# Four padding tiles and wider weight rows: every matmul operand 64 bytes past a multiple of 128

## Chip, cores, metric

One core of a Trainium2 chip runs the kernel; the seven others are idle. The metric is the device time of one execution in microseconds, the median of several runs. Beside it stands one profiled execution, from which every view of the trace comes.

## What is computed

Four residual layers in a row on `x` of 2048 positions by 640 features, A, B, A, B, with a layer norm in front of each. A is a sliding dilated attention, B a two-dimensional Fourier mixing done with matmuls. Cut to what matters:

```python
def _A_ref(x, wqkv, wo):                  # H = 32 heads of 20, window W = 8, dilation 2
    q, k, v = split_heads(x @ wqkv)
    kg, vg = k[idx], v[idx]               # 8 positions: pos, pos-2, ..., pos-14
    logits = einsum("bhsd,bhswd->bhsw", q, kg) * scale
    o = einsum("bhsw,bhswd->bhsd", softmax(masked(logits)), vg)
    return merge_heads(o) @ wo

def _B_ref(x, dft_seq_re, dft_seq_im, dft_hid_re, dft_hid_im):
    a = einsum("bsd,ed->bse", x, dft_hid_re)
    b = einsum("bsd,ed->bse", x, dft_hid_im)
    return einsum("ts,bse->bte", dft_seq_re, a) - einsum("ts,bse->bte", dft_seq_im, b)

x = x + _A_ref(_layernorm(x), wqkv, wo)
x = x + _B_ref(_layernorm(x), ...)
x = x + _A_ref(_layernorm(x), wqkv, wo)
x = x + _B_ref(_layernorm(x), ...)
```

## The kernel before

Every float32 operand of a product is kept as two float32r tiles, a high part `hi` and the rest `lo`, and a product runs as three matmuls: hi x hi, hi x lo, lo x hi (`PASSES`, line 213; the second index is that of the moving operand). A matmul has a stationary operand of 128 x 128 and a moving one of 128 x N, and adds into a PSUM bank.

**Layer A** (`layer_a`) goes over four row blocks c of 512 positions (each four tiles j of 128) and four quarters q of the QKV weights. `qkv_mm` (line 347, matmul on 357) makes one tile of 128 positions by 480 columns: 15 matmuls, k = 0 to 4 in each of the three passes, with the stationary tile `s0` to `s3` (the transposed, normalized input of tile j) and the moving tile `r1_q`, the split weights. There are 128 such tiles in the two layers, 1920 matmuls of 480 columns. The attention itself runs on VectorE, GpSimd and ScalarE (lines 422 to 482). `wo_mm` (line 495, matmul on 504) multiplies by `wo` in products of 320 columns. At the end of the layer `z_mm` of `LayerB` (line 903, matmul on 914) already makes the first sequence product of layer B (t = 0), with the moving tile `ct` in `s0` to `s3` and the stationary tile `r1_c`, which now holds the normalized rows of block c. The order in which all engines work in layer A is written out by hand (`PHASES`, `at`).

**Layer B** first runs `zpart` for t = 1 (16 steps s of 15 matmuls of 512 columns, line 914): the moving tile is `s3` for even s and `s0` for odd s, the stationary tile `r1_c` with c = s // 4. Beside it VectorE makes combined inputs (`x_combine`), which are stored to DRAM through two `stg` buffers. Then come three pairs (`pair`), each with three loops of eight iterations of 512-wide products (`product`, matmul on 1081): 18 matmuls an iteration in the first loop, 21 in the second, 15 in the third. Their moving tiles are split DFT rows in `s0`, `s1` or in cells of `r1_2` and `r1_3`, their stationary tiles either a cell of `r1_0` to `r1_3` read where it stands (`x_plain`) or a combined input loaded into a cell of `r1_0` or `r1_1` (`x_slot`; the ring goes over the eight cells of `r1_0` and `r1_1` in loops 1 and 2, two cells an iteration, and over the four of `r1_1` in loop 3). `ymm` (matmul on 992) multiplies by the hidden-dimension matrices in products of 320 columns, with moving tiles in `r2a`, `pr0` to `pr3` and `zo3`. TensorE's order is written by hand; that of the other engines in layer B is left to the tile scheduler.

**Where tiles lie.** A tile is asked for under a tag. All tiles of a tag share one place; the places follow each other in the order in which the tags are first asked for, each rounded up to 32 bytes (per partition), behind an area of 16384 bytes that is reserved for DMA descriptors and 128 bytes of constants. From this follow the addresses before, as remainders:

| tag | holds, as a matmul operand | start | mod 128 |
|---|---|---|---|
| `ident`, `nident` | matrices of transposes and subtractions | 16544, 17056 | 32 |
| `s3` | input tile j = 3, DFT rows | 17568 | 32 |
| `r1_0` | QKV weights q = 0, rows of block 0 in layer B | 22784 | 0 |
| `pr0` | hidden-dimension weights k = 0 | 43264 | 0 |
| `win` (five buffers) | none | 48384 to 62464 | 0 or 64 |
| `pr1` to `pr3` | hidden-dimension weights | 65984 to 76224 | 64 |
| `r1_1`, `r2a`, `r1_2`, `r1_3` | as `r1_0`, and `wo` | 81344 to 147904 | 64 |
| `zo0` to `zo3`, `ot`, `s0`, `s1`, `s2`, `xa` | stationary tiles, DFT rows | behind | 64 |

Inside a tile all matmul operands start at multiples of 128 bytes from the tile's start (a block of 128 float32 is 512 bytes, a weight row of 480 is 1920 = 15 x 128, one of 320 is 1280). Modulo 256 the weight rows of 480 alternate, since 1920 = 7.5 x 256. The places end at 229312 of the 229376 bytes of a partition.

Of the kernel before, what the change touches and what calls it, by code (L numbers as in the profile page):

```python
# [11 lines left out]
F32R = mybir.dt.float32r  # L12
# [14 lines left out]
P = 128  # L27
# [3 lines left out]
KD = D // P  # L31
F = 160
# [42 lines left out]
def tile_layers(ctx: ExitStack, tc: tile.TileContext, x, wqkv, wo, cs, wre, wim, out):  # L75
    nc = tc.nc
# [9 lines left out]
    def nm(base):  # L86
        uid[0] += 1
        return f"{base}_{uid[0]}"

    def T(shape, tag, dt=F32, bufs=1, pool=None):  # L90
        return (pool or sb).tile(shape, dt, tag=tag, name=nm(tag), bufs=bufs)
# [4 lines left out]
    warm = T([P, 1], "warm")  # L96
    nc.vector.memset(warm, 0.0)
    nc.scalar.activation(warm, warm, AF.Exp)
    ident = T([P, P], "ident")
    make_identity(nc, ident)  # L100
    nident = T([P, P], "nident", F32R)
# [6 lines left out]
    mhalf = T([P, 4], "mhalf")  # L108
    nc.gpsimd.memset(mhalf, -0.5)
    mask = T([P, SLOTS], "mask")  # L110
    nc.gpsimd.memset(mask, 0.0)
    nc.gpsimd.memset(mask[0:2, 0:3], NEG)
    nc.gpsimd.memset(mask[0:1, 3:7], NEG)
# [11 lines left out]
    def split(hi, lo, src, neg=False, eng=None):  # L125
        nc.scalar.activation(hi, src, AF.Copy, scale=-1.0 if neg else 1.0)
        if neg:
            nc.vector.scalar_tensor_tensor(lo, src, -1.0, hi.bitcast(F32), op0=ALU.mult, op1=ALU.subtract)
        else:
            (eng or nc.vector).tensor_tensor(lo, src, hi.bitcast(F32), op=ALU.subtract)  # L130
# [57 lines left out]
    def load_x(src, j, tag="xa"):  # L188
        xt = T([P, D], tag, bufs={"xa": 2}.get(tag, 1))
        nc.sync.dma_start(xt, src[:, j, :])  # L190
        return xt
# [10 lines left out]
    def wq_load1(q, k):  # L202
        raw = wtile([P, 3 * F])
        nc.sync.dma_start(raw, wqkv[q][:, k, :])
        return raw

    def a_weights_q(q):
        wt = T([P, 2, KD, 3 * F], f"r1_{q}", F32R)
        for k in range(KD):
            split(wt[:, 0, k], wt[:, 1, k], wq_load1(q, k))  # L210
        return wt
# [25 lines left out]
    def layer_a(li, stats, handoff, prev):  # L237
# [4 lines left out]
        wq = {}  # L242
# [16 lines left out]
        def at(step, phase, fn, *args):  # L259
            plan.setdefault((step, phase), []).append((fn, args))  # L260
# [5 lines left out]
        def x_load(c, j, tag="xa"):  # L266
            xnT[(c, j)] = load_x(xin[c], j, tag)

        def x_stats(c, j, fast=False):
            if j == 0:  # L270
                stats[c] = Stats()
            stats[c].tile(j, xnT[(c, j)], fast)

        def x_fin(c, j):
            stats[c].finish(j, j + 1)

        def x_norm(c, j, fast=False):
            stats[c].apply(j, xnT[(c, j)], fast)

        def xt_pe(c, j, part, bank):  # L280
            if part == 0:
                xnT[(c, j, 1)] = T([P, 2, KD, P], f"s{j}", F32R)
            xnT[(c, j, "p", part)] = t_pe(xnT[(c, j)], part, bank)

        def xt_hi(c, j, part):
            t_hi(xnT[(c, j, 1)], part, xnT[(c, j, "p", part)])

        def xt_lo(c, j, part):
            t_lo(xnT[(c, j, 1)], part, xnT[(c, j, "p", part)])
# [234 lines left out]
            nstats[c].finish(j0, j1)  # L524

        def wq_begin(q):
            wq[q] = T([P, 2, KD, 3 * F], f"r1_{q}", F32R)

        def wq_raw(q):
            if q < 3:  # L530
                if q == 1:
                    wq["raw"] = T([P, 2, KD, 3 * F], "r2a")
                nc.sync.dma_start(wq["raw"][:, q - 1], wqkv[q])
                for k in range(KD):
                    wq[(q, k)] = wq["raw"][:, q - 1, k]
                return
            for i, tag in enumerate(("zo2", "zo3", "ot")):
                k0, k1 = 2 * i, min(2 * i + 2, KD)
                raw = wq_load(q, k0, k1, tag)
                for k in range(k0, k1):  # L540
                    wq[(q, k)] = raw[:, k - k0]
# [26 lines left out]
        def early():  # L568
            def x_get(j):
                x_load(0, j)  # L570
                x_norm(0, j)

            def w0():
                with tc.issue_after(prev.dma.ins):
                    wq[0] = a_weights_q(0)

            def xt(j, part):
                xt_pe(0, j, part, "pq")
                xt_hi(0, j, part)
                xt_lo(0, j, part)  # L580

            prev.pair(
                NPAIR - 1,
                stats,
                {
                    2: lambda: (x_get(0), x_get(1)),
                    4: lambda: xt(0, 0),
                    5: lambda: (xt(0, 1), x_get(2)),
                    6: lambda: xt(1, 0),
                    7: lambda: (w0(), xt(1, 1), x_get(3)),  # L590
                    ("y", 1): lambda: xt(2, 0),
                    ("y", 2): lambda: xt(2, 1),
                    "end": lambda: (xt(3, 0), xt(3, 1)),
                },
            )
            for q in range(1, NQ):
                wq[q] = a_weights_q(q)
# [7 lines left out]

        def prologue_first():
            wq_begin(0)
            for j, (k0, k1) in enumerate(((0, 3), (3, 5))):
                x_load(0, j, f"pr{j}")
                for k in range(k0, k1):  # L610
                    wq[(0, k)] = wq_load1(0, k)
            for j in range(2, NJ):
                x_load(0, j, f"pr{j}")
            for q in (1, 2, 3):
                wq_begin(q)
                wq_raw(q)
            w0 = wq[0]

            def whi(k, eng):
                (eng.tensor_copy if eng is nc.vector else eng.copy)(w0[:, 0, k], wq[(0, k)])  # L620

            def wlo(k, eng):
                eng.tensor_tensor(w0[:, 1, k], wq[(0, k)], w0[:, 0, k].bitcast(F32), op=ALU.subtract)

            def xt_all(j, bank):
                return [(xt_pe, (0, j, i, f"{bank}{i}")) for i in range(2)] + [
                    (f, (0, j, i)) for i in range(2) for f in (xt_hi, xt_lo)
                ]

            x_stats(0, 0, True)  # L630
            x_fin(0, 0)
            for k in range(3):
                whi(k, nc.scalar)
            wlo(0, nc.vector)
            x_norm(0, 0, True)
            wlo(1, nc.gpsimd)
            for i in range(2):
                xt_pe(0, 0, i, f"t{i}")
            for i in range(2):
                xt_hi(0, 0, i)  # L640
            x_stats(0, 1, True)
            wlo(2, nc.gpsimd)
            x_fin(0, 1)
            whi(3, nc.vector)
            whi(4, nc.vector)
            for i in range(2):
                xt_lo(0, 0, i)
            wlo(3, nc.vector)
            wlo(4, nc.vector)
            x_norm(0, 1, True)  # L650
            x_stats(0, 2, True)
            x_fin(0, 2)
            mid[0] = xt_all(1, "aux") + [(x_stats, (0, 3, True)), (x_fin, (0, 3)), (x_norm, (0, 2, True))]
            mid[1] = xt_all(2, "t") + [(x_norm, (0, 3, True)), (zero_rows, ())]
            mid[2] = xt_all(3, "aux")
            for i in range(KD):
                at(LEAD0[0] + 1 + i // 2, "misc", wq_split, 1, i)
                at(LEAD0[0] + 3 + i, "misc", wq_split, 2, i)
                at(LEAD0[0] + 5 + i, "misc", wq_split, 3, i)
# [31 lines left out]
        while len(gs) < NGRP:  # L691
            if st % 2 == 0 and len(tx) < NC * NJ:
                c, j = divmod(len(tx), NJ)
# [114 lines left out]
        with tc.manual_schedule(engines=ENGINES):  # L808
            if first:
                prologue_first()  # L810
            nc.vector.tensor_copy(mk, mask)
            for s in range(LEAD0[0], last + 1):
                for ph in PHASES:
                    for fn, args in plan.pop((s, ph), ()):
                        fn(*args)
            pc_pe(67)
            pc_hi(67)
            pc_lo(67, True)
            wo_mm(c, 2, None, 0, 2, 3)
            wo_mm(c, 3, ("pq", "aux0"))  # L820
            wo_add(c, 2)
            wo_stats(c, 2)
            wo_fin(c, 2, 3)
            if first:
                handoff.c_hl(14)
            handoff.ln_tail(c, 2, xr, nstats)
            wo_add(c, 3)
            handoff.ln_lo(c, 2)
            handoff.z_mm(14, None)
            wo_stats(c, 3)  # L830
            wo_fin(c, 3, 4)
            if first:
                handoff.c_hl(15)
            handoff.ln_tail(c, 3, xr, nstats)
            handoff.ln_lo(c, 3)
            handoff.z_mm(15, None)
# [478 lines left out]
```

## Time and profile before

| | us |
|---|---|
| median of 3 runs | 1810.0 (1809.1 to 1810.69) |
| span of the profiled execution | 1804.2 |
| TensorE matmul busy in it | 1745.8 (97%) |
| VectorE busy | 1392.7 (77%) |
| ScalarE busy | 818.3 (45%) |
| GpSimd busy | 633.5 (35%) |
| DMA moved | 423.59 MB |

The profile is of one execution; its span runs from the first to the last instruction, and the runs' time also holds what lies around it. PE stands for TensorE's matmuls, PEld for its weight loads, DVE for VectorE, ACT for ScalarE, POOL for GpSimd, SP for the engine that issues most DMAs. Matmuls overlap each other in the pipeline, so one record lasts longer than the distance to the next (383 ns on average for a 480-wide one); what counts for the time is the distance from start to start, which a window with a known number of matmuls shows. The chain of waits is followed back from the last instruction: at each step to what released it, or to the instruction before it on the same engine.

### The profile page before, as it was taken

How to read it: one execution, taken by the hardware profiler on the slowest of the kernel's cores; microseconds unless marked ns; L12 is line 12 of the kernel's file. 1: busy time of each engine (PE TensorE's matmuls, PEld its weight loads, DVE VectorE, ACT ScalarE, POOL GpSimd, SP SyncE). 2: the span in 40 equal slices, each digit the busy share in tenths (PEclk: the TensorE clock that was granted, in tenths of full speed). 3: DMA queues.
4: the chain of work that ended last, by engine and by line, in shares of the span. 5: the costliest groups of instructions: out<-in, count | busy, mean ns of one | idle time of the engine just before them, and what ended most of it. 6: DMA issues, size and time to landing. Idle time of an engine off the chain costs nothing.

```text
span 1804.2 us, 26493 instructions
## 1 busy us (share of the span) xinstructions
PE 1745.8 (97%) x8798; PEld 1506.7 (84%) x8798; DVE 1392.7 (77%) x2135; ACT 818.3 (45%) x1708; POOL 633.5 (35%) x591
## 2 busy tenths in 40 slices
PE   9999997988999999999999999999899999999999
PEld 7879886877888888888888888888788888888888
DVE  5899899887767767768739988899777677677673
ACT  5544644544445445445633334444434443443441
POOL 3799898960000000000008987889400000000000
PEclk9999999999999999999999999999999999999999
DMA  6776667648777887888737856687687767776761
GB/s 233 224 264 206 208 206 250 211 150 293 255 261 247 293 267 248 290 269 267 251 124 227 278 184 198 201 299 260 218 295 262 262 223 228 264 232 229 254 209 52
DMA packets 273994, 423.59 MB, mean 235 GB/s; under 512 B 22688, under 2 KB 153248, under 8 KB 273600
## 3 DMA queue, kind: packets, MB, share of 16 engines
q1 hardware_dynamic: 270656, 419.92, 70.1%
q10 hardware_dynamic: 3200, 1.97, 0.4%
q8 instruction: 70, 1.15, 0.3%
q14 instruction: 68, 0.56, 0.1%
HBM read 336.66 MB, written 85.14 MB: 234 GB/s over the span
## 4 chain that ended last, share of the span: by engine, by line
PE 64%; DVE 15%; DMA 9%; POOL 6%; issue 3%; ACT 3%; SPq 0%; DVEq 0%; ACTq 0%; POOLq 0%
PE m L357 15%; PE aux L992 12%; PE t L1081 10%; PE m L1081 10%; PE pq L1081 5%; PE xt L1081 5%; PE aux L504 4%; DMA xc<-stg 4%; DVE pr L426 3%; DVE pr L464 2%; POOL pr L479 2%; DMA win<-cs_in 1%; POOL pr L428 1%; DVE lg L434 1%; POOL r L864 1%
## 5 line engine op out<-in xcount | busy, mean ns | idle before, releaser
L357 PE MATMUL m<-r,s 128*128 128x480 f32 x1920 | 438.8, 383 | 7.4 <-ACT s L227 3.5
L357 PEld LDWEIGHTS m<-r,s 128*128 128x128 f32 x1920 | 356.1, 189 | 63.5 <-ACT s L227 5.1
L1074 ACT CAST r<-win 128x512 fp32r<-128x512 f32 x251 | 153.0, 620 | 171.8 <-DVE win L1110 73.1
L169 POOL TENSOR_TENSOR stats<-stats,mhalf 128x1 f32<-128x1 f32 (+1 forms) x40 | 29.1, 727 | 566.3 <-ACT stats L165 566.2
L992 PE MATMUL aux<-r2a,zo 128*128 128x320 f32 x768 | 226.4, 310 | 0.0
L479 POOL TENSOR_TENSOR pr<-pr 128x640 f32<-128x640 f32 x126 | 203.5, 1615 | 43.1 <-DVE pr L464 42.1
L426 DVE TENSOR_TENSOR pr<-pq,win 128x1280 f32<-128x1280 f32 x128 | 189.8, 1483 | 26.7 <-ACT pq L399 26.5
L992 PE MATMUL aux<-pr,zo 128*128 128x320 f32 x704 | 208.2, 308 | 0.0
L1075 DVE TENSOR_TENSOR r<-win,r 128x512 fp32r<-128x512 f32 x251 | 169.2, 687 | 48.2 <-ACT r L1074 45.2
L464 DVE TENSOR_TENSOR pr<-pq,win 128x1280 f32<-128x1280 f32 x128 | 190.8, 1491 | 4.5 <-DVE pq L459 0.2
L428 POOL TENSOR_TENSOR pr<-pr 128x640 f32<-128x640 f32 x128 | 183.7, 1435 | 20.2 <-DVE pr L426 17.2
L1081 PE MATMUL m<-r,r 128*128 128x512 f32 x594 | 153.2, 392 | 0.5 <-ACT r L1074 0.3
L992 PEld LDWEIGHTS aux<-r2a,zo 128*128 128x128 f32 x768 | 144.1, 188 | 2.0
L914 PE MATMUL m<-s,r 128*128 128x512 f32 x384 | 121.8, 404 | 17.2 <-DMA s<-c0b 8.9
L1081 PE MATMUL t<-r,r 128*128 128x512 f32 x495 | 134.0, 392 | 0.0
L992 PEld LDWEIGHTS aux<-pr,zo 128*128 128x128 f32 x704 | 132.2, 188 | 2.0
L1081 PEld LDWEIGHTS m<-r,r 128*128 128x128 f32 x594 | 111.2, 188 | 26.1 <-DVE r L1075 0.9
L914 PE MATMUL t<-s,r 128*128 128x512 f32 x384 | 119.0, 398 | 2.4 <-DVE ot L974 2.4
L480 POOL TENSOR_TENSOR pr<-pr 128x320 f32<-128x320 f32 x126 | 114.8, 911 | 9.9
L364 ACT COPY stg<-m 128x480 f32<-128x480 f32 x128 | 70.8, 555 | 98.8 <-PE m L357 87.1
L434 DVE TENSOR_REDUCE lg<-pr 128x64 f32<-128x640 f32 x128 | 103.9, 812 | 11.3 <-POOL pr L428 11.0
L1081 PEld LDWEIGHTS t<-r,r 128*128 128x128 f32 x495 | 93.0, 188 | 21.3
(270 smaller groups left out, 3239.6 us busy)
## 6 DMA issues: line engine op xcount, KB each, us to landing
win<-cs_in SPq DMA_DIRECT2D x358, 256.0 KB, 4.2
r<-xc SPq DMA_DIRECT2D x240, 256.0 KB, 4.4
win<-kvb SPq DMA_DIRECT2D x96, 440.0 KB, 4.9
xa<-cs_in SPq DMA_DIRECT2D x124, 256.0 KB, 4.0
win<-kvb SPq DMA_DIRECT2D x64, 360.0 KB, 4.8
xc<-stg SPq DMA_DIRECT2D x40, 512.0 KB, 3.5
kvb<-stg SPq DMA_DIRECT2D x60, 320.0 KB, 3.8
xr<-xs SPq DMA_DIRECT2D x40, 320.0 KB, 3.1
```

The lines of the kernel that those rows point to most:

```text
L357: nc.tensor.matmul(mt[g][:, : 3 * F], st[:, a, k], wq[q][:, b, k], start=n == 0, stop=n == 14)
L426: nc.vector.tensor_tensor(pr, q, wview(u, jp, 0, [[1, FE]]), op=ALU.mult)
L428: nc.gpsimd.tensor_tensor(pv[:, :, 0:10], pv[:, :, 0:10], pv[:, :, 10:20], op=ALU.add)
L434: nc.vector.tensor_reduce(lgs[u][:, 2 * jp : 2 * jp + 2].rearrange("p j w h -> p (j w h)"), prq.pop((u, jp))[:, :, 0:10], axis=AX.X, op=AL ...
L464: nc.vector.tensor_tensor(pr.rearrange("p j w (h d) -> p j w h d", d=DH), lgs[u][:, 2 * jp : 2 * jp + 2].unsqueeze(4).to_broadcast([P, 2, ...
L479: g.tensor_tensor(pr[:, :, 0:4], pr[:, :, 0:4], pr[:, :, 4:8], op=ALU.add)
L480: g.tensor_tensor(pr[:, :, 0:2], pr[:, :, 0:2], pr[:, :, 2:4], op=ALU.add)
L914: self.last = nc.tensor.matmul(self.z[t][k], self.xn[c][:, a, j, k * P : (k + 1) * P], self.ct[s][:, b], start=s == 0 and i == 0, stop=s = ...
L992: self.last = nc.tensor.matmul(self.ym[e][:, :320], zt[(k, a, ri)][:, j2 * P : (j2 + 1) * P], w[:, e * 320 : (e + 1) * 320], start=(k, a, ...
L1074: nc.scalar.copy(hi, raw)
L1075: nc.vector.tensor_tensor(lo, raw, hi.bitcast(F32), op=ALU.subtract)
L1081: nc.tensor.matmul(bank, w(a, kb), hl[b], start=start and (a, b) == (0, 0), stop=stop and (a, b) == (1, 0),)
```

## The change

Three tiles that nothing uses are asked for under new tags, which moves what comes behind them: `pad0` (8 floats, 32 bytes), `pad1` (40 floats, 160 bytes), `pad2` (16 floats, 64 bytes). The split QKV weights get rows of 512 elements, of which the first 480 are used, so all rows of a tile start at the same remainder of 2048; the tag's place was 20480 bytes already (its other uses need that), and a tile of 2 x 5 x 512 floats fills it exactly. The area reserved for DMA descriptors goes from 16384 to 1024 bytes.

```diff
     nc.scalar.activation(warm, warm, AF.Exp)
+    T([P, 8], "pad0")
     ident = T([P, P], "ident")
...
     mask = T([P, SLOTS], "mask")
+    T([P, 40], "pad1")
     nc.gpsimd.memset(mask, 0.0)
...
     def a_weights_q(q):
-        wt = T([P, 2, KD, 3 * F], f"r1_{q}", F32R)
+        wt = T([P, 2, KD, 512], f"r1_{q}", F32R)[:, :, :, : 3 * F]
...
         def wq_begin(q):
-            wq[q] = T([P, 2, KD, 3 * F], f"r1_{q}", F32R)
+            wq[q] = T([P, 2, KD, 512], f"r1_{q}", F32R)[:, :, :, : 3 * F]
...
             for j, (k0, k1) in enumerate(((0, 3), (3, 5))):
+                if j:
+                    T([P, 16], "pad2")
                 x_load(0, j, f"pr{j}")
...
-    nc = bacc.Bacc("TRN2", target_bir_lowering=False, num_devices=1)
+    nc = bacc.Bacc("TRN2", target_bir_lowering=False, num_devices=1, dynamic_dma_scratch_size=1024)
```

The addresses that follow: `ident` 1216, `nident` 1728, `s3` 2240, `r1_0` 7616, `pr0` 28096, `win` from 33216, `pr1` 50880, and everything behind `pr1` 15104 bytes lower than before. Modulo 128 all tiles that matmuls read start at 64, modulo 256 at 192 (`win`'s five buffers, which no matmul reads, stand at 64 and 0 modulo 128 in turn).

## The prediction

> **What bounds the kernel now.** The page first: the busy shares, the granted clock, then the chain that ended last by engine and by line.
>
> ```profile
> span 1804.2 us, 26493 instructions
> ...
> PE 1745.8 (97%) x8798; PEld 1506.7 (84%) x8798; DVE 1392.7 (77%) x2135; ACT 818.3 (45%) x1708; POOL 633.5 (35%) x591
> ...
> PEclk9999999999999999999999999999999999999999
> ...
> PE 64%; DVE 15%; DMA 9%; POOL 6%; issue 3%; ACT 3%; SPq 0%; DVEq 0%; ACTq 0%; POOLq 0%
> ...
> L357 PE MATMUL m<-r,s 128*128 128x480 f32 x1920 | 438.8, 383 | 7.4 <-ACT s L227 3.5
> ```
>
> ```profile
> by line: PE m L357 14.7%; PE aux L992 12.0%; PE t L1081 10.2%; PE m L1081 10.0%; PE pq L1081 5.1%; PE xt L1081 5.1%; PE aux L504 3.9%; DMA xc<-stg 3.8%; issue 2.9%; DVE pr L426 2.9%; DVE pr L464 2.3%; POOL pr L479 1.7%; DMA win<-cs_in 1.5%;
> ```
>
> TensorE is the bound, at full clock. Three lines hold most of the chain: the QKV products (L357), the hidden-dimension products (L992) and the sequence products (L1081). A stage view then says where TensorE has no slack.
>
> ```profile
> core 0: us, PE busy (x) PEld busy (x) DVE busy (x) ACT busy (x) POOL busy (x), PEclk, DMA share, GB/s
> ...
> 240.00:420.00 180.00, 157.81 (x801) 134.97 (x801) 160.26 (x238) 87.14 (x204) 142.47 (x127) 0.96 0.65 210
> 420.00:480.00 60.00, 59.08 (x285) 49.93 (x285) 45.70 (x67) 24.23 (x42) 0.00 (x0) 1.00 0.85 300
> 480.00:900.00 420.00, 417.00 (x2074) 357.64 (x2073) 309.10 (x505) 212.62 (x397) 5.21 (x6) 1.00 0.78 263
> 900.00:1200.00 300.00, 290.80 (x1520) 257.22 (x1518) 243.27 (x352) 119.62 (x291) 220.94 (x202) 1.00 0.65 210
> ...
> 1375.00:1804.00 429.00, 425.32 (x2161) 369.90 (x2159) 290.44 (x478) 171.68 (x296) 0.00 (x0) 1.00 0.66 219
> ```
>
> In layer B (480 to 900 and from 1375) TensorE idles 3.0 of 420 and 3.7 of 429 us; the next engine, DVE, has 26% free and DMA 22%. There a shorter matmul is a shorter kernel. In layer A TensorE is still on the chain, but from 240 to 420 it idles 22 us, and DVE (89%) sets the pace.
>
> **Does the address of an operand show in the trace?** The change adds no instruction and takes none away; what it can alter is how fast matmuls follow each other. So I looked for matmuls of one shape that differ in addresses alone. The cleanest place is the loop over s in the first stage of layer B (L914): from s = 4 on the stationary tiles stand at remainder 64 (of 128 bytes), and the moving tile is `s0` (remainder 64) for odd s and `s3` (remainder 32) for even s, 15 matmuls each. Second, the first loop of a pair (L1081): its 18 matmuls an iteration all have moving tiles at 64; in iterations 2, 3, 6, 7 the stationary ones are at 64 too, in 0, 1, 4, 5 the ring of `x_slot` gives 12 of the 18 a stationary cell in `r1_0`, at remainder 0.
>
> ```profile
> core 0: us, PE busy (x), PEclk, DMA share, GB/s
> 441.74:445.14 3.40, 3.40 (x16) 1.00 0.71 254
> 445.14:448.64 3.50, 3.50 (x16) 1.00 0.93 337
> 498.22:506.41 8.19, 8.19 (x38) 1.00 0.88 298
> 506.41:514.78 8.37, 8.37 (x38) 1.00 0.86 287
> ```
>
> ```profile
> 640.52 0.68 PE xt L1081 x3
> 641.20 1.36 PE t L1081 x6
> 642.56 0.68 PE pq L1081 x3
> 643.24 1.40 PE m L1081 x6
> 644.63 0.70 PE xt L1081 x3
> 645.33 1.39 PE t L1081 x6
> 646.73 0.70 PE pq L1081 x3
> ```
>
> The first window is an odd s, the second an even one: 3.40/15 = 227 ns a matmul against 3.50/15 = 233 (the counts of a window include the neighbour that reaches into it). The third and fourth are iterations 2 and 3 against 4 and 5 of one pair: 36 matmuls in 8.19 us (227.5 ns) against 8.37 (232.5). The last fence is the chain through the same place of a later pair: 227 ns up to 643.24, then 1.40/6 = 233 when `r1_0` comes in, and the `xt` and half of the `t` matmuls, whose own operands stand at 64, run at 232 as well. So a misaligned neighbour also throws aligned ones out of step.
>
> The 320-wide products (L992, L504) are at their best already, wherever their operands stand:
>
> ```profile
> 659.80 8.82 PE aux L992 x60
> ```
>
> That is 147 ns; with 227 at 512 columns, a column costs 80/192 = 0.417 ns and a matmul 13.5 ns on top. For 480 columns this line gives 213.5.
>
> **The change, part by part.** The descriptor area shrinks by 15360 bytes, a multiple of 128, so by itself it moves no remainder; it makes room. `pad0` (32 bytes) moves `ident`, `nident` and `s3` from 32 to 64; `pad1` (160) moves `r1_0` and `pr0` from 0 to 64; `pad2` (64) gives `pr1` and everything behind it the remainder 64 that it had. After it every matmul operand is at 64. No count of instructions, DMA bytes or waits changes, and the order on TensorE is written by hand in both layers.
>
> *L1081.* By the code a pair has (18+21+15) x 8 = 432 matmuls, 144 of them with a stationary cell in `r1_0` (96 through the rings of loops 1 and 2, 48 through `x_plain` for i < 4): 864 of 2592 over six pairs. The window pair prices 24 of them at 0.18 us, so 36 x 0.18 = 6.5 us. The other bound: all L1081 matmuls at the pace of the aligned window.
>
> ```profile
> L1081 PE MATMUL m<-r,r 128*128 128x512 f32 x594 | 153.2, 392 | 0.5 <-ACT r L1074 0.3
> ...
> L1081 PE MATMUL t<-r,r 128*128 128x512 f32 x495 | 134.0, 392 | 0.0
> ```
>
> ```profile
> L1081 PE MATMUL t<-s,r 128*128 128x512 f32 x6 | 1.5, 389 | 0.0
> ```
>
> The first two rows are the largest L1081 groups of the whole run, mean record 392 ns; the last is a group of the aligned window (498 to 506 us), 389; 3 ns x 2592 = 7.8 us. I take 7.1. L1081's share of the chain is 30.4% of 1804.2 = 548 us of some 2592 x 0.230 = 596, so 0.92 of it is on the path: 6.5 us.
>
> *L914.* In the first stage of layer B (t = 1) 8 blocks of 15 have `s3`, 2 more `r1_0` (s = 1, 3): 20 blocks in two layers at 0.10 us (3.50 - 3.40) are 2.0 us. But the chain there runs through the stores of the combined inputs, DMA xc<-stg, 3.8% = 69 us, about the length of that stage twice over (two `stg` buffers, each held until its store lands). So between 0 and 2.0; I take 1.0. In layer A's tail (t = 0) 7 blocks a layer, 1.4 us, lie in the stretch where TensorE idles 22 of 180 us: nothing.
>
> *L357, alignment.* Four quarters q of the weights; `r1_0` holds q = 0, and `s3` is the stationary tile for j = 3.
>
> ```profile
> 29.59:32.82 3.23, 3.23 (x16) 1.00 0.54 176
> 32.82:36.08 3.26, 3.26 (x16) 1.00 0.53 166
> 36.08:39.35 3.27, 3.27 (x17) 1.00 0.88 288
> ...
> 248.63:251.85 3.22, 3.22 (x16) 1.00 0.47 141
> ```
>
> ```profile
> 207.61 3.30 PE m L357 x15
> ```
>
> Blocks of 15 with both operands at 64 (rows 1, 2, 4) take 215.3, 217.3 and 214.7 ns a matmul, 215.8 on average; `s3` (row 3) 218; `r1_0` (the chain row) 220. An `r1_0` block need not be in this worst rhythm each time, so I take 218.5 for it, midway between 220 and the aligned 217.
>
> *L357, rows of 512.* The trace has no 480-wide stream in rows of 512. In rows of 480 the start moves by 1920 bytes = 7.5 x 256 from k to k, so its remainder of 256 alternates between 64 and 192, which no other product in the kernel does; with rows of 512 it is 192 always, as for L1081 and L992, which keep their step. Below: the 213.5 of the straight line. Above: nothing gained, 215.8, or a loss (a rival, below). I take the middle, 214.6, since the nearest rows, at 320 and 512 columns, sit on the line, but the aligned 480-wide blocks have not reached it once. Then: 1080 matmuls (q > 0, j < 3) x 1.2 + 360 (q > 0, j = 3) x 3.4 + 480 (q = 0) x 3.9 = 1.3 + 1.2 + 1.9 = 4.4 us; bounds 2.1 (at 215.8) and 6.7 (at 213.5). L357 has 14.7% = 265 us of the chain, of 1920 x 0.217 = 417: 0.64, so 2.8 us (1.3 to 4.3). What covers the rest is DVE's and POOL's attention work between 240 and 420 and from 900 to 1200; were it not there, 1.6 us more would show.
>
> *Nothing.* 320-wide products: their moving `pr0` goes from 0 to 64, 147 ns either way. The transposes (`ident`) and the subtractions through `nident`: some 350 short matmuls, between 0 and 350 x 6 ns = 2.1 us, taken as 0, since they sit where TensorE waits for other engines. DMA: `xa` already starts at the same remainder that most tiles get, and lands no slower than `win`, whose five buffers have four different ones:
>
> ```profile
> win<-cs_in SPq DMA_DIRECT2D x358, 256.0 KB, 4.2
> ...
> xa<-cs_in SPq DMA_DIRECT2D x124, 256.0 KB, 4.0
> ```
>
> **Sum.** 6.5 + 1.0 + 2.8 = 10.3 us off the span: 1793.9. The runs lie 5.8 us above the profiled span (1810.0 against 1804.2), so 1799.7.
>
> **Rivals.**
>
> *QKV falls in step (0.22).* With fixed remainders the 480-wide stream reaches 213.5 and, TensorE being quicker, the rest of that saving shows too: 7.1 + 2.0 + 6.7 = 15.8, so 1794. For it: 320 and 512 both lock. Against: 265 of 417 us on the chain, not all.
>
> *Slower: QKV is thrown out of step by the rows of 512 (0.08).* All widths that hold their step are multiples of 64 columns (256 bytes); 480 is 7.5 of them. If the alternating start is what compensates the half, a fixed start costs a half period more on every matmul: up to the 227 ns of a 512-wide one. That is 1920 x (227 - 217) = 19 us, of which 12 (0.64) to all, against 7.5 gained by the others: 1810 - 7.5 + 16 = 1818. It decides from 7.5/(1920 x 0.64) = 6 ns, a spacing of 223. Against it: the worst steady block above is 220, with a stationary tile in step and weights at remainder 0.
>
> *TensorE's gain is taken over by another engine (0.13).* Layer B's DVE chain (subtract, combine, split) and DMA at 78 to 88% become the wait; half of L1081 and half of QKV remain: 3.3 + 1.4 = 4.7, so 1805. Against it: 3 us of idle in 420.
>
> *The addresses are not the cause (0.07).* The even and odd s could differ by something that goes with the buffer. Then 1810. Against it: the two tiles `s3` and `r1_0`, one moving, one stationary, in two loops, give the same 233. The Trainium skill speaks for this rival: in "SBUF — State Buffer", section "Specifications (TRN2)", what costs is crossing 16-byte lines, and 0, 32 and 64 are all starts of such lines, so by that rule the gain is 0 and the time stays 1810; the trace disagrees, with 3.50 against 3.40 us for 15 matmuls.
>
> **How the numbers follow.** 0.50 for the sum (own range 1795 to 1804: L1081 6.0 to 7.2 on the path, L914 0 to 2.0, QKV 0 to 4.3, rounding outwards), the rest as given. Low end 1792: the second case with the transposes. High end 1808: past the third case, without the last two. About 0.2%, 3.6 us, is what a measurement of this kernel tells from no change. Faster: 0.50 + 0.22 + 0.10 of the third = 0.82; same: 0.03 + 0.07 = 0.10; slower: 0.08.
>
> **What would show it.** Blocks of L914 should take 3.40 us for even and odd s alike; 36 matmuls of L1081 8.2 us in every iteration; L1081 records 389 ns on average; blocks of L357 3.22 us or less for 15, the same for all q and j. Layer B (480 to 900) should shorten by about 3.3 us, layer A by 1 to 2 each. I am wrong if L914's even blocks still take 3.50, if L357's blocks pass 3.30, or if TensorE's idle time in layer B grows by as much as its spacing gains.

## The result, and the profile after

| | before | after |
|---|---|---|
| median, us | 1810.69 (1808.63 to 1816.39, 11 runs) | 1804.78 (1802.21 to 1809.4, 11 runs) |
| ratio to before, 95% interval | | 0.9966 [0.9954, 0.9978] |
| span of the profiled execution, us | 1804.2 | 1801.7 |
| TensorE matmul busy in it, us | 1745.8 | 1738.2 |

The changed kernel takes 0.34% less, 6.2 us (1810.69 x 0.0034), with 4.0 to 8.3 us by the interval. The profiled execution after took 1803.44 us, 1.7 more than its span. With that distance the profiled execution before was worth about 1806, quicker than each of its 11 runs, so the difference of the two spans, 2.5 us, understates the gain.

The page of the kernel after: the engines' busy times, the chain by engine, and the largest group of QKV products.

```profile
span 1801.7 us, 26493 instructions
...
PE 1738.2 (96%) x8798; PEld 1506.1 (84%) x8798; DVE 1389.8 (77%) x2135; ACT 817.9 (45%) x1708; POOL 633.2 (35%) x591
...
PE 64%; DVE 15%; DMA 9%; POOL 7%; issue 3%; ACT 3%; SPq 0%; DVEq 0%; ACTq 0%; POOLq 0%
...
L359 PE MATMUL m<-r,s 128*128 128x480 f32 x1920 | 440.9, 384 | 7.0 <-ACT s L229 3.7
...
L1085 PE MATMUL m<-r,r 128*128 128x512 f32 x594 | 151.9, 390 | 0.5 <-ACT r L1078 0.2
...
L1085 PE MATMUL t<-r,r 128*128 128x512 f32 x495 | 133.2, 391 | 0.0
```

The numbers of instructions are the same; lines have moved by 2 in layer A and by 4 in layer B (L357 is now L359, L1081 is L1085, L914 is L918). TensorE is still the bound. The records of the pair products fell (392 to 390 and 391), those of the QKV products did not (383 before, 384 after). The same stretches as before, by stage:

```profile
core 0: us, PE busy (x) PEld busy (x) DVE busy (x) ACT busy (x) POOL busy (x), PEclk, DMA share, GB/s
...
240.00:420.00 180.00, 158.10 (x810) 135.27 (x809) 160.48 (x241) 88.61 (x206) 142.28 (x127) 0.97 0.67 213
420.00:480.00 60.00, 59.40 (x289) 50.32 (x288) 44.76 (x66) 24.00 (x42) 0.00 (x0) 1.00 0.86 300
480.00:900.00 420.00, 415.59 (x2075) 358.51 (x2074) 308.90 (x507) 212.54 (x399) 5.22 (x6) 1.00 0.80 264
900.00:1200.00 300.00, 290.49 (x1508) 256.78 (x1506) 241.76 (x349) 118.16 (x289) 220.78 (x202) 0.99 0.66 208
...
1375.00:1804.00 429.00, 421.62 (x2163) 369.94 (x2161) 290.71 (x480) 171.87 (x298) 0.00 (x0) 1.00 0.68 219
```

In layer B (480 to 900) TensorE now idles 4.4 of 420 us where it idled 3.0, so part of what its matmuls save comes back as waiting; the last window holds the end of the program and can't be compared that way. Now the cleanest places again, TensorE alone. First an odd s of the first stage of layer B, an even s, then iterations 2 and 3, and 4 and 5, of one pair; behind them four QKV blocks of 15 (the third has `s3`).

```profile
core 0: us, PE busy (x), PEclk, DMA share, GB/s
...
438.88:442.28 3.40, 3.40 (x17) 1.00 0.61 231
442.28:445.68 3.40, 3.40 (x17) 1.00 0.96 341
497.93:506.09 8.16, 8.16 (x37) 1.00 0.82 266
506.09:514.25 8.16, 8.16 (x37) 1.00 0.85 270
...
29.67:32.92 3.25, 3.25 (x16) 1.00 0.52 154
32.92:36.17 3.25, 3.25 (x17) 1.00 0.58 186
36.17:39.42 3.25, 3.25 (x16) 1.00 0.93 294
248.65:251.89 3.24, 3.24 (x16) 1.00 0.49 133
```

The even s takes 3.40 us where it took 3.50, iterations 4 and 5 take 8.16 where they took 8.37: both slow cases are gone. The QKV blocks are alike now, 3.24 to 3.25, but at 216.7 ns a matmul (3.25/15), not faster than the aligned ones before (3.22 to 3.26).

The records overlap, so I also took the distance from the start of each matmul to the start of the next, over the whole trace and with waits left out, and sorted it by the remainder of 256 bytes of (start of the moving operand minus start of the stationary one); in brackets stands how many of the pair products have that remainder:

```
mean start-to-start, ns          before                after
pair products, 512 columns   0: 228.55 (1728)      0: 227.2 (2592)
                           192: 233.24 (864)
L914 (after: L918), 512      0: 228.4              0: 228.3
               160, 192, 224: 232.8 to 233.3
QKV, 480 columns             0: 216.4              0: 216.9
                           128: 216.0
                        others: 216.5 to 219.4
```

The 320-wide products are as before within 0.3 ns (L992 146.9 ns, after, as L996, 146.6). A difference of 256 bytes modulo 512 costs nothing: after, the pair products take 227.2 ns with it and without it. So the remainder of 256, and not of 512, is what to sort by.

### The profile page after: what moved, and what is told of

Same layout as the page of the kernel before. It is cut to its first block, busy times and chain, and to the rows that moved or that the text cites. A ratio compares the mean times of both kernels' runs of the same rounds, so it can differ in the third digit from the quotient of the medians.

```text
span 1801.7 us, 26493 instructions
## 1 busy us (share of the span) xinstructions
PE 1738.2 (96%) x8798; PEld 1506.1 (84%) x8798; DVE 1389.8 (77%) x2135; ACT 817.9 (45%) x1708; POOL 633.2 (35%) x591
## 4 chain that ended last, share of the span: by engine, by line
PE 64%; DVE 15%; DMA 9%; POOL 7%; issue 3%; ACT 3%; SPq 0%; DVEq 0%; ACTq 0%; POOLq 0%
PE m L359 16%; PE aux L996 12%; PE t L1085 10%; PE m L1085 10%; PE pq L1085 5%; PE xt L1085 5%; DMA xc<-stg 4%; PE aux L506 4%; DVE pr L428 3%; DVE pr L466 3%; POOL pr L481 2%; POOL pr L430 2%; DMA win<-cs_in 2%; POOL r L868 1%; POOL pr L482 1%
## 5 line engine op out<-in xcount | busy, mean ns | idle before, releaser
L359 PE MATMUL m<-r,s 128*128 128x480 f32 x1920 | 440.9, 384 | 7.0 <-ACT s L229 3.7
L359 PEld LDWEIGHTS m<-r,s 128*128 128x128 f32 x1920 | 357.5, 189 | 63.9 <-ACT s L229 5.5
L996 PE MATMUL aux<-r2a,zo 128*128 128x320 f32 x768 | 226.0, 309 | 0.0
L996 PE MATMUL aux<-pr,zo 128*128 128x320 f32 x704 | 207.8, 309 | 0.0
L1085 PE MATMUL m<-r,r 128*128 128x512 f32 x594 | 151.9, 390 | 0.5 <-ACT r L1078 0.2
L996 PEld LDWEIGHTS aux<-r2a,zo 128*128 128x128 f32 x768 | 144.3, 188 | 2.0
L918 PE MATMUL m<-s,r 128*128 128x512 f32 x384 | 120.1, 400 | 16.8 <-DMA s<-c0b 8.2
L996 PEld LDWEIGHTS aux<-pr,zo 128*128 128x128 f32 x704 | 132.2, 188 | 2.1
L1085 PE MATMUL t<-r,r 128*128 128x512 f32 x495 | 133.2, 391 | 0.0
L1085 PEld LDWEIGHTS m<-r,r 128*128 128x128 f32 x594 | 111.5, 188 | 24.5 <-DVE r L1079 1.0
L918 PE MATMUL t<-s,r 128*128 128x512 f32 x384 | 116.7, 392 | 2.4 <-DVE ot L978 2.4
L1085 PEld LDWEIGHTS t<-r,r 128*128 128x128 f32 x495 | 93.4, 189 | 20.0
```

What stands on the lines that cost most here:

```text
L359: nc.tensor.matmul(mt[g][:, : 3 * F], st[:, a, k], wq[q][:, b, k], start=n == 0, stop=n == 14)
L918: self.last = nc.tensor.matmul(self.z[t][k], self.xn[c][:, a, j, k * P : (k + 1) * P], self.ct[s][:, b], start=s == 0 and i == 0, stop=s = ...
L996: self.last = nc.tensor.matmul(self.ym[e][:, :320], zt[(k, a, ri)][:, j2 * P : (j2 + 1) * P], w[:, e * 320 : (e + 1) * 320], start=(k, a, ...
L1085: nc.tensor.matmul(bank, w(a, kb), hl[b], start=start and (a, b) == (0, 0), stop=stop and (a, b) == (1, 0),)
```

## Experiments

Two questions: which property of the addresses gives the gain, and where TensorE's saving stops short of the end. Ratios are to the kernel before, run on the same chip, with a 95% interval.

### Which part of the change: the pads or the rows

`e1_pads_only` is the kernel after with weight rows of 480; `e2_rows_only` is the kernel before with rows of 512.

```diff
# e1_pads_only, against after (both places)
-        wt = T([P, 2, KD, 512], f"r1_{q}", F32R)[:, :, :, : 3 * F]
+        wt = T([P, 2, KD, 3 * F], f"r1_{q}", F32R)
# e2_rows_only, against before (both places)
-        wt = T([P, 2, KD, 3 * F], f"r1_{q}", F32R)
+        wt = T([P, 2, KD, 512], f"r1_{q}", F32R)[:, :, :, : 3 * F]
```

> The three pads and the smaller descriptor area, but QKV weights in rows of 480 as before. Theory: all of the gain is alignment to 64, and the rows of 512 give nothing; then QKV blocks (L359's matmuls) average about 216 ns from start to start, a shade under the 216.9 of the changed kernel, L1081 stays at 227, and the time is that of the changed kernel or up to 1 us less: ratio to before 0.996 to 0.997. Rival: the fixed row start is what the QKV blocks need; then they stay at 217 to 218 and the time is 1 to 3 us above the changed kernel's (ratio 0.998).

> Before with the rows of 512 alone, all remainders of 128 as before. Theory: QKV blocks with both operands at 64 go from 216.2 to 216.7 ns, those with s3 or r1_0 stay at 218 to 220, the 512-wide products are as before (227 and 233): time within 0.1% of before. Rival: rows of 512 carry part of the gain: blocks of QKV under 216 and the time 1 to 3 us under before.

e1: 1803.42 us, 0.9972 [0.996, 0.9984]. e2: 1809.48 us, 1.0005 [0.9994, 1.0015]. So the pads (there are three, not the four of the title) are the whole change; the rows of 512 are worth nothing that can be measured. The same four QKV blocks in e1, TensorE alone:

```profile
29.69:32.92 3.23, 3.23 (x16) 1.00 0.52 155
32.92:36.17 3.25, 3.25 (x16) 1.00 0.58 186
36.17:39.40 3.23, 3.23 (x16) 1.00 0.95 301
248.30:251.55 3.25, 3.25 (x16) 1.00 0.48 134
```

3.23 and 3.25 with rows of 480, against 3.24 and 3.25 with rows of 512. Over all 1920 the mean distance is 216.2 ns in e1 and 216.9 after.

### Which remainder: 64, any, or an equal one

`e3_all_zero` puts every operand at remainder 0 of 128, `e5_all_32` at 32. `e6_r10_off128` leaves every operand at 64 of 128 and moves `r1_0` (and `pr0`) alone by 128 bytes, so that it differs from the rest modulo 256.

```diff
# e3_all_zero, against after
-    T([P, 8], "pad0")
+    T([P, 24], "pad0")
...
-    T([P, 40], "pad1")
+    T([P, 8], "pad1")
# e5_all_32, against after
-    T([P, 8], "pad0")
+    T([P, 32], "pad0")
...
-    T([P, 40], "pad1")
+    T([P, 8], "pad1")
# e6_r10_off128, against after
-    T([P, 40], "pad1")
+    T([P, 72], "pad1")
...
-                    T([P, 16], "pad2")
+                    T([P, 48], "pad2")
```

> The changed kernel with pads such that every matmul operand starts at remainder 0 of 128 instead of 64. Theory (the value 64 counts): 512-wide products run at 233 ns everywhere, blocks of L914's loop 3.50 us for even and odd s, so L1081 is 3 ns a matmul slower than before: +7 us in it, the time 5 to 12 us above before (ratio 1.003 to 1.007). Rival (equal remainders count, whichever): 227 ns and 3.40 us as in the changed kernel, ratio 0.997.

> The same with every matmul operand at remainder 32 of 128. Theory (64 counts): 233 ns everywhere as at 0, ratio 1.003 to 1.007. Rival (equal remainders count): 227 ns, ratio 0.997. A mixed outcome, slow at 0 and quick at 32 or the other way round, would say that something else than 64 against not 64 decides.

> The changed kernel with 128 bytes more ahead of r1_0 and 128 more behind pr0: r1_0 and pr0 start at 64 modulo 256, all other operands at 192 modulo 256; every operand is still 64 past a multiple of 128. Theory (moving and stationary must be equal modulo 256): the 864 pair matmuls with a stationary cell in r1_0 run at 233 ns and throw their neighbours out of step, the mean of L1085 is 230 ns as in the kernel before, even and odd s blocks of L918 differ no more (3.41 us from s = 4 on) but s below 4 takes 3.50; time 2 to 5 us above the changed kernel's, ratio to before 0.998 to 0.9995. Rival (64 past a multiple of 128 is enough): 227 ns everywhere, ratio 0.997.

e3: 1804.87 us, 0.9969 [0.9958, 0.9981]. e5: 1803.09 us, 0.9967 [0.9954, 0.998]. e6: 1811.03 us, 1.0000 [0.9988, 1.0012]. The value 64 does not matter: 0 and 32 do as well. But 64 everywhere is not enough either: e6 keeps it and loses the whole gain. The windows of e3, in the order of those above (odd s, even s, iterations 2 and 3, iterations 4 and 5):

```profile
439.73:443.15 3.42, 3.42 (x16) 1.00 0.65 237
443.15:446.64 3.49, 3.49 (x16) 1.00 0.99 345
496.53:504.69 8.16, 8.16 (x37) 1.00 0.88 303
504.69:512.85 8.16, 8.16 (x37) 1.00 0.87 279
```

and those of e6:

```profile
438.67:442.07 3.40, 3.40 (x17) 1.00 0.71 245
442.07:445.47 3.40, 3.40 (x17) 1.00 0.97 343
494.87:503.04 8.17, 8.17 (x37) 1.00 0.83 278
503.04:511.39 8.35, 8.35 (x37) 1.00 0.85 269
```

In e3 the even s is slow again, though `s3` and `r1_c` both stand at 0 of 128: they stand 128 bytes apart modulo 256. In e6 it is iterations 4 and 5 that are slow, and there it is `r1_0` that stands 128 bytes off. Sorted as above, the pair products of e6 take 228.1 ns at distance 0 and 232.8 at distance 128 (864 of them, as before), those of e3 and e5 227.2 throughout. What counts is that moving and stationary operand start at the same remainder of 256 bytes. Each slow window has one operand that does not; a difference of 128 costs as much as the 192 that the pairs had before. `pr0`, which moves along with `r1_0` in e6, is no rival: its 320-wide products take 146.8 ns at distance 128, the others 146.6.

### Which operand: `r1_0` or `s3`

`e11_r10_alone` is the kernel after without `pad0`: `s3`, `ident` and `nident` go back to 32, `r1_0` and all the rest stay.

```diff
-    T([P, 8], "pad0")
...
-    T([P, 40], "pad1")
+    T([P, 48], "pad1")
```

> The changed kernel without pad0: s3, ident and nident stay at 32 past a multiple of 128 as before, r1_0 and everything else as in the changed kernel. Theory (s3's slower matmuls lie in layer B's first stage and layer A's tail, which TensorE does not bound): blocks of L914's loop with even s take 3.50 us again, QKV blocks with j = 3 218 ns, yet the time is within 1.5 us of the changed kernel's, ratio 0.9966 to 0.9975. Rival (s3 carries its 3 us share of the spacing): ratio 0.998 to 0.999.

1806.51 us, 0.9972 [0.996, 0.9984]. Odd s and even s in its trace:

```profile
440.75:444.15 3.40, 3.40 (x16) 1.00 0.67 238
444.15:447.65 3.50, 3.50 (x16) 1.00 0.92 337
```

The even s costs its 0.10 us again and the ratio stands within the interval of the full change. e3 and e5, which also leave `s3` 128 bytes off, say the same with their full gain. So what can be measured of the gain is `r1_0`'s; e6 shows it from the other side, with `s3` aligned and `r1_0` not. Of the 8.1 us of spacing by which e6 lies above after, 6.5 are in the pair products, the rest is in L918 and in the QKV products with `r1_0`.

### Can a third `stg` buffer or two more `win` buffers add to it

The smaller descriptor area leaves 15104 bytes. `e4_stg3` gives `stg` a third buffer (first stage of layer B, where the chain runs through DMA xc<-stg). `e8_win7` is e1 with seven `win` buffers for five, `e7_stg3_win7` is e1 with both.

```diff
# e4_stg3, against after (every place that asks for stg)
-            hl = T([P, 2, 2, 256], "stg", F32R, bufs=2)
+            hl = T([P, 2, 2, 256], "stg", F32R, bufs=3)
# e8_win7, against e1_pads_only; e7_stg3_win7 has this and the above
-NWIN = 5
+NWIN = 7
...
-                    T([P, 16], "pad2")
+                    T([P, 48], "pad2")
```

> The changed kernel with three stg buffers instead of two (the freed space holds the third). Theory (in layer B's first stage the chain runs through stg's two buffers and their stores, so quicker matmuls there only wait longer at the head of pair 0): the combined inputs are stored earlier, the stage and pair 0 together take 1 to 2.5 us less in each layer B, ratio to before 0.994 to 0.996. Rival (the head of pair 0 waits for VectorE's queue and the loads of DFT rows, not for stg): the stage is as in the changed kernel, ratio 0.997.

> Pads only (rows of 480), with three stg buffers and seven win buffers instead of five. Theory (the time saved on TensorE is given back where layer B waits for loads into win and for stg): more of the 10 us that the spacing saves shows, ratio to before 0.991 to 0.995. Rival (what gives it back are the clock and engines' queues): 0.996 to 0.998 as for pads alone.

> Pads only with seven win buffers, stg at two. Theory that loads into win hold TensorE up: half or more of what e7_stg3_win7 gains over pads alone, 0.993 to 0.996. Rival (stg alone holds it up): 0.997 as pads alone.

A gain was expected of each, and all are slower than before: e4 1814.59 us, 1.0021 [1.0011, 1.0032]; e7 1818.21 us, 1.004 [1.0025, 1.0056]; e8 1815.45 us, 1.0027 [1.0016, 1.0038]. The waits of e4 from 420 to 490 us (total, times, longest) show where:

```profile
PEld aux L996 <- ACT zo L128: 6.4, 1, 6.4
PE aux L996 <- ACT zo L128: 6.1, 1, 6.1
```

TensorE waits once, 6.1 us, for the last split of the hidden-dimension weights. In the order that the tile scheduler gives VectorE and ScalarE with three buffers, combined inputs stand ahead of that split, and the first stage of layer B takes 82.4 us for 75.6 in the kernel after. In e8 it is pair 0 of the first layer B that grows, 136.9 us for 130.6; what holds it up there is not shown.

### Can the order be mended

`e9_stg3_w_first` is e4 with the first combined inputs queued behind that split; `e10_w_first` has the same order with two `stg` buffers, as after. `e12_evac_first` is the kernel after with one combined input of pair 0 queued behind the last subtraction that empties the first stage's result out of PSUM.

```diff
# e9_stg3_w_first against e4, e10_w_first against after
-                split(hl[0], hl[1], raw, neg=True)
+                self.wlast = split(hl[0], hl[1], raw, neg=True)
...
-                        for fn, args in todo[:3]:
-                            fn(*args)
+                        with tc.issue_after(self.wlast.ins):
+                            for fn, args in todo[:3]:
+                                fn(*args)
# e12_evac_first, against after (zlast: the last subtraction of the first stage)
-                    c7 = split(combine(b22, b21, b22, ALU.add))
+                    if p == 0 and i == 0:
+                        with tc.issue_after(self.zlast.ins):
+                            b22 = combine(b22, b21, b22, ALU.add)
+                        c7 = split(b22)
```

> The changed kernel with three stg buffers, and the combined inputs of layer B's first stage queued on VectorE behind the last split of the hidden-dimension weights. In e4_stg3 TensorE waited 6 us for that split inside the stage and took 2 us less at the head of pair 0. Theory: with the split first, the stage is back at 75 to 77 us and pair 0 keeps its 2 us: 3 to 4 us under the changed kernel, ratio to before 0.994 to 0.996. Rival: the late start of the combined inputs moves the wait to pair 0's head again, 0.997 or more.

> The same order, with stg at two buffers. Theory (two buffers and their stores set when the combined inputs are all stored; starting them later makes them end later): pair 0's head waits longer than in the changed kernel, ratio 0.998 to 1.001. Rival (the order of the splits is what counts, not the buffers): as e9_stg3_w_first.

> The kernel after, with one change of order at the head of pair 0: the combine that makes c7 (L1114, which waits for the DMA xa<-cs_in) is queued on VectorE behind the last subtraction that takes the first stage's result out of PSUM (L978, ot<-t), on which TensorE's t matmul waits. Theory (the hand-over at the head of pair 0 gives back part of the gain because that subtraction stands behind a combine that waits for a load): TensorE's wait for ot falls from 2.2 us to under 1.2, the stretch of matmuls at half clock behind it is gone, pair 0 takes 128 to 129 us in the first layer B where after takes 130.6 and before 129.3, and the ratio to before is 0.994 to 0.9955. Rival (the wait moves on to the next product, whose combined input now comes later, or the scheduler's new order of VectorE loses it elsewhere): pair 0 stays at 130 us or more and the ratio at 0.9966 or above.

e9: 1806.15 us, 0.9974 [0.9963, 0.9985]. e10: 1816.78 us, 1.0032 [1.0017, 1.0047]. e12: 1812.52 us, 1.0004 [0.9989, 1.0019]. e9 has its first stage back at 75.9 us, but its pair 0 takes 133.7 us, after's 130.6: the wait has moved by one stage. In e10, which is slower than either side of its expectation, it is 136.1, in e12 134.5. The timeline of e12 at the head of pair 0, VectorE and TensorE, says why (start, duration, what; in brackets the idle time before):

```profile
488.05 0.69 DVE L1118 TENSOR_TENSOR xa<-win,xa 128x512 f32<-128x512 f32 x1 [1.72 <-issue]
488.66 0.88 DVE L1013 TENSOR_TENSOR xr<-aux,xr 128x320 f32<-128x320 f32 x2
489.46 0.41 DVE L980 TENSOR_TENSOR ot<-t,zo 128x256 fp32r<-128x256 f32 x1
...
490.02 0.92 PE L1089 MATMUL t<-r 128*128 128x512 f32 x3 [2.26 <-DVE ot L980]
492.30 1.98 PE L1089 MATMUL t<-r,r 128*128 128x512 f32 x3 [1.35 <-ACT r L1082]
```

The combine that was moved is gone from in front of the subtraction (L980), but the scheduler put another there (L1118, `xa`), VectorE idles 1.72 us ahead of it (the trace names no releaser), and TensorE waits 2.26 us as it did. A second wait of 1.35 us has come, for the operand whose combine now runs later. Behind the two waits 11 matmuls run at half the granted clock, 427 ns each (13 at the same place of the second layer B). The rival held: the wait moves on. Whether the gain grows with that subtraction truly first is not shown, since no kernel had it so.

## Why the prediction came out, step by step

Forecast were 1799.7 us (10.3 us less) in a range of 1792 to 1808; measured 1804.78 (6.2 us less by the ratio). The direction and the cause, addresses and nothing else, held. The size came out at 0.6 of the forecast: the measured time is just past the upper end of the sum's own range (1795 to 1804), and one term of the sum, below, was worth nothing. The number of the third rival, 1805, is nearer, but not its account: no other engine took half of QKV's gain, since QKV's products gained nothing.

*L1081, predicted 7.1 us of spacing, 6.5 on the path: right in the spacing, and near on the path.* Summed matmul by matmul, the starts of the pair products moved together by 7.4 us between the two traces. Where the pairs run without a wait, all of it arrives. The durations of the stages of layer B, from the first start of one to the first start of the next, each from the one profiled execution of its kernel (B1 and B2 are the two layers B; a pair 2 ends with its last product, and the start of the second A is the 415 matmuls behind that):

```
us                    before    e2  | after    e1     e3     e5
B1 first stage          76.3   76.5 |  75.6   75.2   75.0   75.5
B1 pair 0              129.3  129.8 | 130.6  130.5  129.7  128.4
B1 pair 1              136.9  137.3 | 137.0  136.6  136.1  135.8
B1 pair 2              133.7  134.4 | 132.3  133.1  132.3  132.4
start of second A       80.1   81.1 |  83.1   82.6   82.6   81.4
B2 first stage          75.6   75.8 |  76.1   76.9   76.6   75.1
B2 pair 0              126.8  127.7 | 126.6  127.1  127.1  126.1
B2 pair 1              134.6  134.6 | 133.3  133.3  133.3  134.0
B2 pair 2              132.9  132.9 | 131.5  131.8  131.5  131.5
```

The last two pairs lose 1.3 us each, as the third of the first layer B does: 144 slow matmuls and their neighbours a pair, 7.1/6 = 1.2 by the prediction. All six pairs together take 794.1, 796.7 and 797.1 us where `r1_0` stands off (before, e2, e6) and 788.1 to 792.3 where it doesn't (after, e1, e3, e5, e11), on average 796.0 and 790.8: 5.2 us on the path, by eight single executions. The first pair of the first layer B has next to none of it (130.1 against 129.9).

*L914, predicted 0 to 2.0, taken as 1.0: the lower bound was the right one.* Its spacing gained 2.4 us, but e11 gives most of it back, 1.8 us (the blocks with `s3`: the eight even s of each layer and four in each layer A's tail), without a measurable loss. The reading that the stores of the combined inputs set the end of that stage is in line with it.

*L357, alignment, predicted as part of 4.4: right in kind, and small.* Blocks with `r1_0` took 218.7 ns before and those with `s3` 218.0, the rest 216.2. Aligned and with rows of 480 (e1) they take 216.2 on average. From the 217.0 of all 1920 before, that is 0.8 ns each, 1.5 us of spacing; the rows of 512 take 0.7 of the 0.8 back.

*L357, rows of 512, taken as 214.6 ns: wrong, and the step that failed.* It took the middle between 213.5, where a line through the 320- and 512-wide products puts 480 columns, and 215.8. Measured are 216.9, past the bound for no gain: an operand start that steps by whole 256 bytes does not bring a 480-wide matmul to that line, and the kernel with rows of 480 is no worse. What the whole QKV term came to is (217.0 - 216.9) x 1920, 0.2 us of spacing, where 4.4 was put. (Its upper bound of 6.7 adds up to 6.5 from its own rows, 1080 x 2.3 + 360 x 4.5 + 480 x 5.0 ns, and the short matmuls are 428, not some 350; the sum rests on neither.) Without QKV's 2.8 us on the path and with L914 at nothing the sum is 6.5, inside the measured 4.0 to 8.3.

*That the cause is the value modulo 128 (all at 64): too narrow a reading.* The trace before did not separate 64 everywhere from equal remainders; e3, e5 and e6 did. The case that the addresses are not the cause falls by e6 alone. It also settles the rule of the Trainium skill that the prediction weighed, in "SBUF — State Buffer", "Specifications (TRN2)": the cost there comes with crossing 16-byte lines, and between e6 and the kernel after all starts of lines stay starts of lines, yet 8.35 us stand against 8.16.

*The third case, that another engine takes over half of the gain: in part, at one place.* In the table the kernel after is no quicker than before in pair 0 of the first layer B, and 3 us slower at the start of the second layer A; the first is such a case, the second isn't. The timeline of the kernel after at the head of pair 0, TensorE and then VectorE:

```profile
487.06 0.84 PE L1085 MATMUL xt<-r 128*128 128x512 f32 x3
490.12 1.18 PE L1085 MATMUL t<-r 128*128 128x512 f32 x3 [2.22 <-DVE ot L978]
491.10 1.49 PE L1085 MATMUL t<-r,r 128*128 128x512 f32 x3
492.38 1.49 PE L1085 MATMUL pq<-r,r 128*128 128x512 f32 x3
...
488.55 0.69 DVE L1114 TENSOR_TENSOR win<-xa,win 128x512 f32<-128x512 f32 x1 [1.41 <-DMA xa<-cs_in]
489.16 0.48 DVE L1009 TENSOR_TENSOR xr<-aux,xr 128x320 f32<-128x320 f32 x1
489.56 0.41 DVE L978 TENSOR_TENSOR ot<-t,zo 128x256 fp32r<-128x256 f32 x1
```

The same place before:

```profile
489.88 0.86 PE L1081 MATMUL xt<-r 128*128 128x512 f32 x3
491.88 0.92 PE L1081 MATMUL t<-r 128*128 128x512 f32 x3 [1.14 <-DVE ot L974]
492.63 0.86 PE L1081 MATMUL t<-r,r 128*128 128x512 f32 x3
493.34 0.86 PE L1081 MATMUL pq<-r,r 128*128 128x512 f32 x3
```

TensorE comes 2.8 us earlier (487.06 against 489.88) and waits 1.1 us longer, for a subtraction that stands on VectorE's queue behind a combine, which itself waits for the load of `xa`. Then three matmuls take 1.28 us (491.10 to 492.38), 427 ns each, where they took 0.71 us before. The second place is the start of the second layer A; first after, then before:

```profile
911.97 5.52 PE L359 MATMUL m<-r,s 128*128 128x480 f32 x13 [0.57 <-ACT s L229]
```

```profile
914.20 3.11 PE L357 MATMUL m<-r,s 128*128 128x480 f32 x13 [0.57 <-ACT s L227]
```

The wait is the same 0.57 us, yet 13 matmuls take 5.52 us for 3.11; 11 of them start 400 ns apart. The granted clock (PEclk) in the two places after shows it:

```profile
490.50:493.70 3.20, 3.20 (x10) 0.52 0.80 220
912.00:917.40 5.40, 5.40 (x14) 0.51 0.01 3
```

Half the clock, for some 3 and 5 us. At the second place it was there in the traces of after, e1, e3, e5 and e11 (6 to 12 matmuls) and of e2 (7, two matmuls further on), and not in those of before and e6. The Trainium skill ("TensorE: Matmul & The Clock Gate", "What's actually happening") has the clock at half rate behind a free-running window of about 3.4 us in which TensorE was idle. The 0.51 and 0.52 agree with the half rate; the single wait of 2.22 us in front of the first place is shorter than such a window.

The clock records of the 14 traces tell what brings the stretch about. The clock changes only on a grid of 3.413 us, which lies differently to the program in each execution. From 30 us on it falls to half 106 times, each time behind a grid interval of which matmul records cover 0.52 or less; of the 7012 intervals behind which it stays full, none is covered less than 0.43. So a wait of about half an interval is enough, if it falls into one. The interval ahead of the first place after, and the one at the same place before:

```profile
487.22:490.64 3.42, 1.20 (x6) 1.00 0.16 57
```

```profile
488.58:491.99 3.41, 2.27 (x11) 1.00 0.25 96
```

After, 1.20 of 3.42 us are covered (0.35), since the longer wait lies wholly in it; before, the wait of 1.14 us leaves 2.27 of 3.41 (0.67) covered, and no position of the grid would have made it less. So at pair 0 the earlier arrival does make half the clock likelier: the waits there are 1.30 to 2.22 us in after, e1, e3, e5 and e11, of which after and e1 fell, and 1.14 to 1.49 in before, e2 and e6, of which none did. At the start of the second layer A the waits are alike, 1.82 and 0.57 us before and 1.86 and 0.57 after, and by an estimate from those of before two thirds of the grid's positions bring half the clock. It fell in e2 too, without the change's addresses, and stayed full in e4, e9 and e12, which have them and take 80.2 to 80.7 us there. So most of the 3 us of that row is luck of the executions that were profiled, and not a price of the change. What such stretches cost the medians is not shown; the sum without QKV fits them with no loss at the hand-overs at all.

*That the runs lie 5.8 us above the span.* They lie 1.7 to 1.9 above their own span; the 5.8 compared a quick execution with the median of others. It did the sum no harm, since adding it back amounts to taking 10.3 us off the median.

The slower rival, QKV thrown out of step to a spacing of 223 ns and more, didn't come: 216.9 after, and the rows alone (e2) leave the time as it was. QKV falling in step to 213.5 didn't either.

## What to carry to other kernels

Where matmuls follow each other without a wait, start the moving and the stationary operand at the same remainder of 256 bytes: here it was worth 6 ns of 233 on each mismatched 512-wide float32r matmul and on average 1.4 on the matched ones between them, for 256 bytes of padding. Look for such an effect in windows of equal work that differ in buffers alone, and extrapolate a spacing to another width only where a block of that width has reached it. A saving on the bounding engine arrives whole in stages where it never waits; at a hand-over behind another engine's queue it can turn into waiting, and more buffers there can make it worse, since they change the order in which a scheduler lets the other engines work. Before a slow stretch in one trace is put down to a change, read its granted clock, and the same place in other traces.

## What the runs showed of the hardware

The cost of unequal starts does not grow with the distance: 128, 160, 192 and 224 bytes modulo 256 all give 232.4 to 233.3 ns in 512-wide products (224 is 32 bytes the other way round, the smallest offset that occurs), equal starts 227.2 to 228.6. The 480-wide products behave otherwise: 216.0 ns at a distance of 128 with rows of 480 (before), but 218.8 with rows of 512 (e6). At 320 columns nothing is lost: 147.0 ns at equal starts and 145.8 at a distance of 64 before, 146.6 and 146.8 at 0 and 128 in e6.

Aligned 480-wide blocks with rows of 512 run in two rhythms within a trace, a cycle of four matmuls at about 215, 218, 216 and 217 ns or one of two at 212 and 221; both average 216.6. The line through 320 and 512 columns, 213.5, is not reached by either.

The granted clock falls to half behind an interval of its 3.413 us grid that is covered by matmuls about half or less (0.52 at most in 106 falls), not only behind one that is idle throughout.
